# Routed attention and a SERF feed-forward on one core: GpSimd's in-weight forms started three pairs earlier, and the first in-projection's side work laid out anew

## The chip, the core and the metric

The kernel runs on one core of one Trainium2 chip. The core has TensorE (PE; its weight loads are shown as PEld), VectorE (DVE), ScalarE (ACT), GpSimd (POOL) and SyncE (SP), which work through queues of their own and wait for each other by semaphores. The metric is the device time of one execution in microseconds (us). Every profile in this document is of one execution, and times within it are us from the start of its span.

## The reference

Queries and keys are assigned to one of 16 centroids of their head; a query attends to the keys of its own cluster alone. The result is put into rows of 512 numbers and goes through a feed-forward whose activation is h * erf(softplus(h)).

```python
batch, n_heads, seq, head_dim = (4, 8, 768, 64)      # n_clusters = 16
q_assign = np.argmax(np.einsum('bhsd,hcd->bhsc', q_n, c_n), axis=-1)
k_assign = np.argmax(np.einsum('bhsd,hcd->bhsc', k_n, c_n), axis=-1)
mask = q_assign[:, :, :, None] == k_assign[:, :, None, :]
scores = np.where(mask, scale * np.matmul(q, k.transpose(0, 1, 3, 2)), -1000000000.0)
attn = np.exp(scores - np.max(scores, axis=-1, keepdims=True))
attn = attn / (np.sum(attn, axis=-1, keepdims=True) + 1e-09)
x = np.matmul(attn, v).transpose(0, 2, 1, 3).reshape(B * S, H * D)   # 3072 x 512
h = x @ w_in                                          # 512 x 2048
g = h * erf(np.maximum(h, 0.0) + np.log1p(np.exp(-np.abs(h))))
out = g @ w_out                                       # 2048 x 512
```

## The kernel before

**Order of the work.** Nearly every instruction goes through a small class (`InOrder`, L119-132) that records it and keeps each engine in program order; so the profile puts almost all of them on L127, and tiles' names tell them apart. What an engine does next is the order in which the program issues it. DMAs that are issued by `nc.sync` directly are not bound in that way, and stand in SP's queue where the scheduler that builds the program puts them.

**Attention.** 16 pairs of heads (p = 0 to 15), six periods each (i = 0 to 5, `period`, L1367). A period computes scores of two blocks of keys (tile `sc`), their exponentials (ACT, `pr<-sc`), the products with the values (PE, `turned<-pr,in_v`) and, on GpSimd, a running sum of the exponentials (`accumulate`, `more_out<-more_out,pr`). At the end of each half of a pair `divide` (L593) sums that over rows on PE (`turned<-more_out,minus`), takes a reciprocal on ACT (logarithm, exponential), and scales on DVE (`den`, two steps in `turned`, `more_out<-den,turned`); SP stores the result to `x_dram`.

**Weights.** Beside the attention the weights are brought in and made ready for the multiplication by steps that round and rescale them: `fetch` (SP), `size` and `rest` (ACT), `bounded` (DVE), `sign` (ACT), `shifted` (DVE), `summed` (GpSimd, which also issues the next `fetch`). The list `w_steps` (L280) has 16 steps for `w_in`, by column blocks of 512 in the order 0, 512, 1024, 1536, and 16 for `w_out`; pair p finishes steps 2p-2 and 2p-1. The last four (`N_LATE`) are done after the attention, in the first in-projection.

**Forms.** The feed-forward multiplies 2x2 blocks by a scheme of seven products (`ORDER`, L695 and on: 1, 2, 6, 7, 5, 3, 4), which needs sums and differences of blocks of both factors ("forms", 128x512 each). `left_forms` gives four forms for a pair of column blocks f of `w_in`, `right_forms` four for x. In `before`, three groups of four in-weight forms are listed as (DVE, GpSimd) choices; GpSimd takes one from the list in period 1 of each pair named in `POOL_FORMS` (L47: pairs 8 to 15), DVE takes 1, 2, 2 and 2 in periods 0, 3, 4 and 5 of pair 15 (`FORMS`, L46). The four forms of x are put at the end of that list after pair 13; what is left of it goes to DVE behind the loop, and the fourth group of in-weight forms goes to GpSimd behind the attention (L1552).

**First in-projection.** `hidden(0, 0)` and `hidden(0, 1)` (L741) work on one chunk of 512 rows, four column blocks j each, seven products per j. One product is called a block here: four matmul records on PE into one PSUM bank, then one or two operations that add the bank to the results `g`. Blocks are numbered 0 to 55 over both calls. From block 7 on eight banks are used in turn, six of a pool and the two tiles `turned`; in the first seven, six of the pool. For the first product of each j, `hidden(0, 0)` copies by ACT (`first=ae.copy`), `hidden(0, 1)` by DVE. After each block one entry of the list `aside_work` is issued; an `idle` entry is empty. In `before` that list holds: three idle, the four late weight steps (`weights`, sixteen entries), `first_half` (ACT's softplus and erf of half of g, tile `a_s`), `all_sums` (four `summed` on GpSimd), two entries of `middle_forms26` (GpSimd), three idle, the four products `g<-a_s,g` on DVE (`first_products`), and then `second_half`, `late_forms26` (three), four idle, four products. After block 6 `finish_attention` (the rest of the last `divide`) and `next_forms26` are issued. `last_half` is called after the second j of `hidden(0, 1)`: it empties the list and puts in the next half's curves, six idle entries, three left steps and four products.

**Forms of w_out.** The second factor of the out-projection needs its own forms. `early_forms26`, `next_forms26`, `middle_forms26` and `late_forms26` (L816-865) make them on GpSimd in that order; `next_forms26` begins with a tile that `divide` uses until its last step. `late_forms26` ends with two adding DMAs from GpSimd (`onto_by_dma`, `more_out<-x_own`).

**Out-projection.** `project26(0)` (L1236) has 26 products of eight matmul records each, numbered p = 0 to 25 here as in the code. `RIGHT` (L62) says which right factor each takes; values of 100 and over are tiles that are made as it goes (`rest_of_forms26`, L867, by p). Four of them matter below. y0 and y1 (tile `x_own`) are made by a fill or a negation and an adding DMA from GpSimd (`x_own<-more_out`) and also stored by SP (`b_dram<-x_own`). The ring tile used at p = 16 is filled by SP (`g_more<-w_out`, after y0's store in SP's queue) and then added to by GpSimd's DMA (`g_more<-x_own`). The same place is filled again for p = 25 and added to (`g_more<-more_out`).

Of the kernel before, what the change touches and what calls it, by code (L numbers as in the profile page):

```python
# [36 lines left out]
DM, DFF = H * D, 2048  # L37
# [5 lines left out]
LC = 512  # L43

UP = 2.0**16
FORMS = {15: {0: 1, 3: 2, 4: 2, 5: 2}}  # L46
POOL_FORMS = {p: (1,) for p in range(8, 16)}  # L47
BIG = 2.0**60
FLOOR = 2.0**50
EPS = 2.0**-70  # L50
# [1 line left out]
N_LATE = 4  # L52
# [83 lines left out]
def kernel(  # L136
# [141 lines left out]


    w_steps = []  # L280
    for c in range(0, DFF, LC):
        for r in range(DM // P):
            w_steps.append((w_in[:, r, c : c + LC], moe_w_in[r * P : (r + 1) * P, 2 * c : 2 * (c + LC)]))
    for f in range(HF):
# [368 lines left out]
    def left_forms(engine, a11, a12, a21, a22, new):  # L653

        return [
            functools.partial(plus_of, new[0], a21, a22, engine),
            functools.partial(minus_of, new[1], new[0], a11, engine),
            functools.partial(minus_of, a21, a11, a21, engine),
            functools.partial(minus_of, new[2], a12, new[1], engine),
        ]  # L660

    def right_forms(engine, b11, b12, b21, b22, new):

        return [
            functools.partial(minus_of, new[0], b12, b11, engine),
            functools.partial(minus_of, new[1], b22, new[0], engine),
            functools.partial(minus_of, b12, b22, b12, engine),
            functools.partial(minus_of, new[2], new[1], b21, engine),
        ]
# [10 lines left out]
    def w_in_parts(f, n):  # L680
        c1, c2 = slice(f * P, (f + n) * P), slice((HF + f) * P, (HF + f + n) * P)
        return (
            w_in[:, 0:HK, c1], w_in[:, HK:, c1], w_in[:, 0:HK, c2], w_in[:, HK:, c2],
            [more_in[:, i, :, c1] for i in range(3)],
        )

    def x_parts(n):
        x = x_of[n]
        return (
            x[:, 0:HK, 0:HT], x[:, 0:HK, HT:], x[:, HK:, 0:HT], x[:, HK:, HT:],  # L690
            [x_more[:, i] for i in range(3)],
        )
# [4 lines left out]
    aside_work = []  # L697
# [60 lines left out]
    def idle(n):  # L758
        return [lambda: None] * n
# [61 lines left out]
    def next_forms26():  # L821
        w, y = w_block, form_places(1)
        store_form(3, ring[0])
        formed_whole(slot(2), w(5), slot(1), 1)
        formed(y[0], w(3), w(7), -1, 0)
        formed(y[1], w(6), w(7), -1, 0)
        formed(slot(0), w(1), w(7), 1, 0)
# [110 lines left out]
    def split_gate(lot, half):  # L938
        products_of = []

        def curves():
            soft, erf, products = gate26(0, lot, half)
            run(f() for f in soft + erf)
            products_of.extend(products)

        return curves, [lambda i=i: products_of[i]() for i in range(4)]
# [411 lines left out]
            run(steps)  # L1358
        return steps

    forms = []
    for f in range(0, HF - 2, 2):
        forms += zip(*(left_forms(e, *w_in_parts(f, 2)) for e in (ve, ge)))
    routing = [iter(())]
    part = [iter(())]
# [1 line left out]
    def period(p, i):  # L1367
        u = 2 * NJ * p + 2 * i
        n1, n2 = 2 * p - 1, 2 * p
        early = lambda n: 0 <= n < N_EARLY  # L1370

        def mask(place):
            which = (MASKS if p else FIRST_MASKS).get((i, place))
            if which:
                return masks(p + 1, *which, turned[0 if i in (0, 5) else 1], place == 2)
            return lambda: None

        if u > 0:
            for which in turns if i in (0, 3) else ():
                turn(*which)  # L1380
                turns.remove(which)
            if i == 3 and not p:
                transposes(2, "k")
            if i == 3 and p:
                similarities(p + 2)
                routing[0] = choose(p + 2, turned[0], True)
            step_ahead(p, 2 * i)
            if i == 3 and p:
                next(routing[0], None)
            if i == 2:  # L1390
                transposes(p + 2, "k" if p else "q")
        mask(0)()
        if i == 0 and early(n1 - 1):
            sign(n1 - 1)
        elif i == 3 and early(n1):
            sign(n1)
        if i == 4:
            next(routing[0], None)
        next(part[0], None)
        if i == 0 and p:  # L1400
            run(routing[0])
            transposes(p + 2, "q")
        if u == 2:
            next(routing[0])
        products(u)
        mask(3)()
        products(u + 1)
        mask(1)()
        second = step_ahead(p, 2 * i + 1, True) if u > 0 else iter(())
        next(second, None)  # L1410
        rows = D if u == 0 or u + NJ + 2 >= len(units) else Q
        scores(u, rows)
        next(second, None)
        next(second, None)
        next(part[0], None)
        if i == 5 or u == 2:
            next(routing[0], None)
        scores(u + 1, rows)
        later = mask(2)
        if i == 3 and not p:  # L1420
            similarities(p + 2)
            routing[0] = choose(p + 2, turned[0], True)
        if i == 0:
            later()
            curve(u)
        else:
            curve(u)
            later()
        curve(u + 1)
        if u == 0:  # L1430
            step_ahead(0, 1)
            similarities(1)
            routing[0] = choose(1, turned[1])
            next(routing[0])
            vectors(1, "q")
            vectors(1, "k")
        if i == 0 and early(n1 - 1):
            bounded(n1 - 1)
            shifted(n1 - 1)
        elif i == 1 and early(n1):  # L1440
            size_and_rest(n1)
        elif i == 5 and early(n2):
            rest(n2)
        for _ in range(min(len(forms), FORMS.get(p, {}).get(i, 0))):
            forms.pop(0)[0]()
        if i == 3:
            if not p:
                next(routing[0], None)
            if early(n1):
                bounded(n1)  # L1450
                shifted(n1)
        elif i == 1:
            load(p + 1, "v", v, vp)
            if p == 0:
                run(routing[0])
        elif i == 4:
            vectors(p + 2, "k")
            vectors(p + 2, "q")
        if u > 0:
            if i == 1 and early(n1 - 1):  # L1460
                summed(n1 - 1)
            elif i == 4 and early(n1):
                summed(n1)
            if i in POOL_FORMS.get(p, ()) and forms:
                forms.pop(0)[1]()
            for w in (u - 2, u - 1):
                accumulate(w)
            for w in (u - 2, u - 1):
                attend(w)
            if i == 3:  # L1470
                next(routing[0], None)
            if i % HJ == 0:
                part[0] = divide(u - 1)
                next(part[0])
        if i == 3 and early(n2):
            size(n2)
# [61 lines left out]
    for p in range(NPAIR):  # L1538
        for i in range(HJ * 2):
            period(p, i)  # L1540
        if p == LAST_X:
            load_x(0)
        if p == LAST_X + 2:
            forms += zip(*(right_forms(e, *x_parts(0)) for e in (ve, ge)))
    for work, _ in forms:
        work()
    u = len(units)
    for w in (u - 2, u - 1):
        accumulate(w)
    for w in (u - 2, u - 1):  # L1550
        attend(w)
    last = divide(u - 1)  # L1552
    for work in left_forms(ge, *w_in_parts(HF - 2, 2)):
        work()
    attention.close()

    psb = pool("psb", 6, space=PSUM)
# [6 lines left out]
    def finish_attention():  # L1564
        run(last)
        banks[:] = [None] * 6 + turned
# [12 lines left out]
    def weights(n):  # L1579
        return [functools.partial(w, N_EARLY + n) for w in (size_and_rest, bounded, sign, shifted)]  # L1580

    def all_sums():
        for n in range(N_LATE):
            summed(N_EARLY + n)
        take_places(2)

    first_half, first_products = split_gate(0, 0)
    second_half, second_products = split_gate(0, 1)
    aside_work += (
        idle(3) + sum((weights(n) for n in range(N_LATE)), []) + [first_half, all_sums, *middle_forms26(), *idle(3), *first_products]  # L1590
    )
    hidden(0, 0, {0: lambda: (finish_attention(), next_forms26())})

    def last_half():
        finish_aside()
        first_steps = [functools.partial(left_step, 0, x) for x, step in enumerate(LEFT_STEPS) if step[0] < 0]
        aside_work.extend(gate_work(0, 1, 0, first_steps, 6))

    aside_work += [second_half, *late_forms26(), *idle(4), *second_products]
    hidden(0, 1, {1: last_half}, first=ve.tensor_copy)  # L1600
    finish_aside()
    project26(0)
    last_of_x = x_more[:, 2, 0, 0:1]
# [42 lines left out]
```

## Time and profile before

| | |
|---|---|
| median of 3 runs | 950.37 us (950.34 to 950.56) |
| the profiled execution's own time | 950.65 us |
| its span | 948.9 us |
| PE busy, at granted clock 1.0 | 939.7 us |
| DVE, ACT, POOL busy | 789.1, 546.5, 504.6 us |
| attention | about 20 to 401 us |
| first in-projection | about 401 to 452 us |
| first out-projection | about 452 to 497 us |

PE's busy time is from the start of each matmul to a modelled end, so that a busy PE may still be held back; where it matters, the number of matmuls in a stretch is read beside it. In the timeline rows the columns are start, duration, engine, line, operation, result<-operands, shape, count, and in brackets the idle time before the row and what ended it. SPq rows are SP's issues of DMAs, not their transfers.

### The profile page before, as it was taken

To read this page: it belongs to the slowest core of one execution; us is meant where nothing else is said; L and a number is where in the kernel's file an instruction comes from. 1 tells how busy PE (TensorE), PEld (TensorE's weight loads), DVE (VectorE), ACT (ScalarE), POOL (GpSimd) and SP (SyncE) were. 2 spreads that over 40 slices of the span, in tenths; PEclk is the share of its full clock that TensorE was granted. 3 is DMA by queue.
4 is the path that set the end of the run, shared out by engine and by line. 5 is a ranking of instruction groups with operands and counts; after the bars stand their busy time and mean duration, and the time that the engine had idled before them with its cause. 6 is when DMAs were issued, how large, how long until landed. Compare 5 with 4: busy or idle time off the path is not lost.

```text
span 948.9 us, 22319 instructions
## 1 busy us (share of the span) xinstructions
PE 939.7 (99%) x8756; PEld 707.2 (75%) x8756; DVE 789.1 (83%) x1417; ACT 546.5 (58%) x809; POOL 504.6 (53%) x357
## 2 busy tenths in 40 slices
PE   8999999999999999999999999999999999999998
PEld 3555555555555555588888888998999899989987
DVE  8888888888888887879886688688868977897887
ACT  3677777777777776476523643654257236525541
POOL 1688888888888888899108211360063016103600
PEclk9999999999999999999999999999999999999999
DMA  9344554444443621132876347353444336343433
GB/s 220 69 114 113 112 113 113 111 113 111 113 112 68 156 56 36 26 120 112 220 209 248 111 117 203 123 180 111 157 158 143 133 115 209 113 153 123 156 112 111
DMA packets 176344, 123.17 MB, mean 130 GB/s; under 512 B 132592, under 2 KB 143344, under 8 KB 176240
## 3 DMA queue, kind: packets, MB, share of 16 engines
q1 hardware_dynamic: 171872, 116.34, 42.5%
q0 software_dynamic: 1872, 4.98, 2.9%
q8 instruction: 69, 1.13, 0.5%
q10 hardware_dynamic: 2496, 0.43, 0.2%
q14 instruction: 35, 0.29, 0.1%
HBM read 91.78 MB, written 23.33 MB: 121 GB/s over the span
## 4 chain that ended last, share of the span: by engine, by line
PE 93%; DVE 2%; ACT 2%; issue 1%; POOL 1%; DMA 1%; SPq 0%; DVEq 0%; POOLq 0%; ACTq 0%
PE bank L127 40%; PE turned L127 31%; PE sc L127 16%; PE wide L127 6%; POOL more_out L127 1%; DVE nmx L127 1%; DVE g L127 1%; ACT a_s L127 0%; DMA g_more<-in_moe_w_out_dram 0%; ACT L127 0%; ACT osb L127 0%; ACT w_out L127 0%; SPq L127 0%; DMA qm<-least_rows 0%; ACT g_more L127 0%
## 5 line engine op out<-in xcount | busy, mean ns | idle before, releaser
L127 POOL TENSOR_TENSOR more_out<-more_out,pr 128x768 f32<-128x768 f32 x128 | 217.6, 1700 | 17.1 <-ACT pr L127 7.5
L127 DVE TENSOR_REDUCE nmx<-wide 128x2 f32<-128x512 f32 (+2 forms) x189 | 179.1, 948 | 47.1 <-PE wide L127 46.0
L127 ACT ACTIVATE pr<-sc 128x768 f32<-128x768 f32 x192 | 148.4, 810 | 81.3 <-PE wide L127 73.3
L127 PE MATMUL turned<-pr,in_v 128*32 128x193 f32 x3072 | 145.2, 330 | 0.0
L127 POOL TENSOR_TENSOR g<-g 128x512 f32<-128x512 f32 x36 | 47.1, 1309 | 180.8 <-DVE g L127 178.9
L127 PEld LDWEIGHTS turned<-pr,in_v 128*32 128x32 f32 x3072 | 90.2, 109 | 51.3 <-issue 26.9
L127 DVE TENSOR_TENSOR g<-g 128x512 f32<-128x512 f32 x132 | 90.8, 688 | 22.3 <-PE bank L127 11.8
L127 PE MATMUL sc<-qT,kT 64*128 64x384 f32 x528 | 98.5, 485 | 0.0
L127 DVE TENSOR_TENSOR g<-bank,g 128x256 f32<-128x256 f32 (+1 forms) x128 | 64.7, 531 | 16.1 <-PE bank L127 9.5
L127 PE MATMUL bank<-g_more,g 128*128 128x256 f32 x320 | 75.7, 379 | 0.0
L127 PE MATMUL bank<-x_own,w_in 128*128 128x128 f32 (+1 forms) x440 | 74.0, 310 | 0.0
L127 ACT ACTIVATE a_s<-g 128x1024 f32<-128x1024 f32 x38 | 39.5, 1054 | 57.4 <-POOL g L127 45.6
L127 POOL TENSOR_TENSOR more_out<-pr,pr 128x768 f32<-128x768 f32 x32 | 59.1, 1848 | 20.0 <-ACT pr L127 19.9
L127 DVE TENSOR_TENSOR g<-a_s,g 128x512 f32<-128x512 f32 x76 | 68.2, 916 | 0.9 <-ACT a_s L127 0.9
L127 PEld LDWEIGHTS bank<-g_more,g 128*128 128x128 f32 x320 | 60.7, 190 | 8.6 <-DVE g L127 0.4
L127 PEld LDWEIGHTS bank<-x_own,w_in 128*128 128x128 f32 x440 | 63.1, 191 | 4.6 <-issue 0.6
L127 PE MATMUL wide<-kv,qv 64*128 64x256 bf16 (+2 forms) x378 | 64.8, 327 | 0.9 <-ACT km L127 0.6
L127 PE MATMUL bank<-w_out,g 128*128 128x256 f32 x280 | 64.5, 379 | 0.0
L127 ACT ACT_TABLE_LOAD x40 | 51.3, 1283 | 19.8 <-DVE g L127 19.2
L127 PEld LDWEIGHTS <-qv 64*128 64x128 bf16 x384 | 23.1, 93 | 52.7 <-issue 37.9
L127 PE MATMUL wide<-km,qm 64*128 64x256 bf16 (+4 forms) x378 | 62.2, 326 | 0.0
L127 PEld LDWEIGHTS sc<-qT,kT 64*128 64x128 f32 x528 | 46.3, 187 | 19.0 <-issue 2.0
(240 smaller groups left out, 1992.6 us busy)
## 6 DMA issues: line engine op xcount, KB each, us to landing
g_more<-b_dram SPq DMA_DIRECT2D x52, 512.0 KB
g_more<-w_dram SPq DMA_DIRECT2D x84, 256.0 KB
x_own<-in_moe_w_in_dram SPq DMA_DIRECT2D x13, 512.0 KB
in_v<-in_v_dram SPq DMA_DIRECT2D x32, 192.0 KB
x_dram<-more_out SPq DMA_DIRECT2D x128, 48.0 KB
x_own<-x_dram SPq DMA_DIRECT2D x6, 1024.0 KB
in_k<-in_k_dram SPq DMA_DIRECT2D x59, 96.0 KB
in_q<-in_q_dram SPq DMA_DIRECT2D x58, 96.0 KB
```

Source lines behind the costliest of these rows:

```text
L127: ins = getattr(self.engine, name)(*args, **kw)
```

## The change

GpSimd takes one in-weight form in period 1 of pairs 5 to 15 instead of 8 to 15. The order of the `w_in` steps puts columns 0 and 1024 first, so that the first two groups' weights are there earlier. All four groups of in-weight forms are in one list (16), and x's four forms have a list of their own, which DVE takes first in pair 15, followed by three in-weight forms; none is left for DVE behind the loop. The two in-weight forms that remain go to GpSimd behind `next_forms26`; the four that stood before `early_forms26` are gone from there. In the first in-projection the late weight steps begin one block earlier (after block 2), `first_half`, `all_sums` and `middle_forms26` too; the products of the first half stand after blocks 25, 27, 29 and 31 instead of 26 to 29; `second_half` after block 33 instead of 30, `late_forms26` after 34 to 36 instead of 31 to 33, its products after 41, 42, 44 and 45 instead of 38 to 41. `last_half` no longer empties the list and is called one j earlier, so its entries follow the earlier ones: curves after block 46 instead of 42, left steps after 53 to 55 instead of 49 to 51, and the four products after the last block instead of after 52 to 55.

```diff
--- before.py
+++ after.py
@@ -44,7 +44,7 @@
 
 UP = 2.0**16
 FORMS = {15: {0: 1, 3: 2, 4: 2, 5: 2}}
-POOL_FORMS = {p: (1,) for p in range(8, 16)}
+POOL_FORMS = {p: (1,) for p in range(5, 16)}
 BIG = 2.0**60
 FLOOR = 2.0**50
 EPS = 2.0**-70
@@ -278,7 +278,7 @@
 
 
     w_steps = []
-    for c in range(0, DFF, LC):
+    for c in (0, DFF // 2, LC, DFF // 2 + LC):
         for r in range(DM // P):
             w_steps.append((w_in[:, r, c : c + LC], moe_w_in[r * P : (r + 1) * P, 2 * c : 2 * (c + LC)]))
     for f in range(HF):
@@ -1358,8 +1358,8 @@
             run(steps)
         return steps
 
-    forms = []
-    for f in range(0, HF - 2, 2):
+    forms, x_forms = [], []
+    for f in range(0, HF, 2):
         forms += zip(*(left_forms(e, *w_in_parts(f, 2)) for e in (ve, ge)))
     routing = [iter(())]
     part = [iter(())]
@@ -1441,8 +1441,8 @@
             size_and_rest(n1)
         elif i == 5 and early(n2):
             rest(n2)
-        for _ in range(min(len(forms), FORMS.get(p, {}).get(i, 0))):
-            forms.pop(0)[0]()
+        for _ in range(FORMS.get(p, {}).get(i, 0)):
+            x_forms.pop(0)() if x_forms else forms.pop(0)[0]()
         if i == 3:
             if not p:
                 next(routing[0], None)
@@ -1541,17 +1541,13 @@
         if p == LAST_X:
             load_x(0)
         if p == LAST_X + 2:
-            forms += zip(*(right_forms(e, *x_parts(0)) for e in (ve, ge)))
-    for work, _ in forms:
-        work()
+            x_forms += right_forms(ve, *x_parts(0))
     u = len(units)
     for w in (u - 2, u - 1):
         accumulate(w)
     for w in (u - 2, u - 1):
         attend(w)
     last = divide(u - 1)
-    for work in left_forms(ge, *w_in_parts(HF - 2, 2)):
-        work()
     attention.close()
 
     psb = pool("psb", 6, space=PSUM)
@@ -1584,20 +1580,29 @@
             summed(N_EARLY + n)
         take_places(2)
 
+    def spread(work):
+        return sum(([w, *idle(1)] for w in work), [])
+
     first_half, first_products = split_gate(0, 0)
     second_half, second_products = split_gate(0, 1)
     aside_work += (
-        idle(3) + sum((weights(n) for n in range(N_LATE)), []) + [first_half, all_sums, *middle_forms26(), *idle(3), *first_products]
+        idle(2) + sum((weights(n) for n in range(N_LATE)), []) + [first_half, all_sums, *middle_forms26(), *idle(3)]
     )
-    hidden(0, 0, {0: lambda: (finish_attention(), next_forms26())})
+    aside_work += spread(first_products)
+
+    def next_forms():
+        next_forms26()
+        for _, work in forms:
+            work()
+
+    hidden(0, 0, {0: lambda: (finish_attention(), next_forms())})
 
     def last_half():
-        finish_aside()
         first_steps = [functools.partial(left_step, 0, x) for x, step in enumerate(LEFT_STEPS) if step[0] < 0]
         aside_work.extend(gate_work(0, 1, 0, first_steps, 6))
 
-    aside_work += [second_half, *late_forms26(), *idle(4), *second_products]
-    hidden(0, 1, {1: last_half}, first=ve.tensor_copy)
+    aside_work += [second_half, *late_forms26(), *idle(4), *second_products[:2], *idle(1), *second_products[2:]]
+    hidden(0, 1, {0: last_half}, first=ve.tensor_copy)
     finish_aside()
     project26(0)
     last_of_x = x_more[:, 2, 0, 0:1]
```

The order of instructions of the two built programs differs in these ways on top: in SP's queue y1's store now stands ahead of the ring tile's fill in the first out-projection; ACT has `size` and `rest` of the second late step ahead of the last `divide`'s logarithm.

## The prediction

> **What bounds the kernel now.** I read the page first.
>
> ```profile
> PE 939.7 (99%) x8756; PEld 707.2 (75%) x8756; DVE 789.1 (83%) x1417; ACT 546.5 (58%) x809; POOL 504.6 (53%) x357
> ```
>
> TensorE works nearly all the time, so an edit on DVE, ACT or POOL changes the time only where PE waits for it. I therefore looked for such waits in the stages that the change touches, in PE's timeline of the first in-projection and then in DVE's and ACT's.
>
> ```profile
> 431.55 1.03 PE L127 MATMUL bank<-x_more,w_in 128*128 128x256 f32 x4
> 432.41 1.89 PE L127 MATMUL bank<-x_own,w_in 128*128 128x256 f32 x8
> 434.69 1.13 PE L127 MATMUL turned<-x_more,more_in 128*128 128x256 f32 x4 [0.40 <-DVE g L127]
> 436.37 1.13 PE L127 MATMUL turned<-x_own,w_in 128*128 128x256 f32 x4 [0.55 <-DVE g L127]
> 437.34 1.03 PE L127 MATMUL bank<-x_more,more_in 128*128 128x256 f32 x4
> ```
> ```profile
> 426.61 0.42 DVE L127 TENSOR_TENSOR g<-turned,g 128x256 f32<-128x256 f32 x1 [2.91 <-ACT g L127]
> ...
> 434.23 0.41 DVE L127 TENSOR_TENSOR g<-turned,g 128x256 f32<-128x256 f32 x1
> 434.56 1.42 DVE L127 TENSOR_TENSOR g<-a_s,g 128x512 f32<-128x512 f32 x1
> 435.90 0.41 DVE L127 TENSOR_TENSOR g<-turned,g 128x256 f32<-128x256 f32 x1
> ```
> ```profile
> 408.44 0.68 ACT L127 ACTIVATE w_out<-g_more 128x512 f32<-128x512 f32 x1 [3.24 <-DMA g_more<-in_moe_w_out_dram]
> 409.02 2.09 ACT L127 ACTIVATE g_more<-g_more 128x512 int32<-128x512 uint32 x2
> 410.83 0.43 ACT L127 ACTIVATE more_out<-turned,alleps 128x192 f32<-128x192 f32 x1
> ...
> 426.23 0.35 ACT L127 COPY g<-turned 128x256 f32<-128x256 f32 x1
> ```
>
> A block starts 0.86 us after the one before (431.55 to 432.41). From 431.55 to 437.34 lie five blocks (the x8 row is two), so 4.30 us would do where 5.79 pass: **the stall costs 1.49**. PE waits there for evictions of the banks `turned` at 434.23 and 435.90; these are late because DVE first waited 2.91 for ACT's copy at 426.23, and then had one of the products, 1.42, before nearly every eviction. ACT's copy is late because ACT has worked without a gap since the late weights landed at 408.44.
>
> The second chain to watch is GpSimd's, from the attention to the out-projection, and the DMAs behind it.
>
> ```profile
> 404.76 1.72 POOL L127 TENSOR_TENSOR more_in<-w_in 128x512 f32<-128x512 f32 x1
> ...
> 410.26 2.90 POOL L127 TENSOR_TENSOR more_out<-w_out 128x512 f32<-128x512 f32 x2
> ...
> 415.79 2.88 POOL L127 TENSOR_TENSOR more_out<-w_out,more_out 128x512 f32<-128x512 f32 x2
> ...
> 422.70 2.73 POOL L127 TENSOR_TENSOR w_out<-w_out,g_more 128x512 int32<-128x512 int32 x2
> ...
> 449.98 1.86 POOL L127 DMA_DIRECT2D more_out<-x_own  x2
> 459.29 0.84 POOL L127 DMA_DIRECT2D x_own<-more_out  x1 [7.46 <-DMA x_own<-w_out]
> ...
> 473.80 0.84 POOL L127 DMA_DIRECT2D g_more<-x_own  x1 [10.23 <-DMA g_more<-w_out]
> 488.77 0.86 POOL L127 DMA_DIRECT2D g_more<-more_out  x1 [14.14 <-PE bank L127]
> ```
> ```profile
> 463.97 0.32 SPq L794 DMA_DIRECT2D b_dram<-x_own  x1
> ...
> 465.79 1.16 SPq L810 DMA_DIRECT2D g_more<-w_out  x1
> 467.90 0.38 SPq L794 DMA_DIRECT2D b_dram<-x_own  x1
> ...
> 478.29 0.32 SPq L794 DMA_DIRECT2D b_dram<-g_more  x1
> ...
> 494.98 0.32 SPq L794 DMA_DIRECT2D b_dram<-g_more  x1
> ```
> ```profile
> 479.72 1.89 PE L127 MATMUL bank<-g_more,g 128*128 128x256 f32 x8
> ...
> 495.26 1.89 PE L127 MATMUL bank<-g_more,g 128*128 128x256 f32 x8
> ```
>
> POOL has no gap between 404.76 and its DMA issues at 449.98, and then waits only for transfers. SP stores a finished ring tile at 478.29 and 494.98, as soon as it is there. PE takes these tiles at 479.72 (p = 16) and 495.26 (p = 25). So the chain has **1.43 us of slack at p = 16 and 0.28 at p = 25**, and nowhere does PE wait for it yet.
>
> **The change, part by part.** *Three more pairs with a form on GpSimd.* Pair 8 has the first one; a pair without and that pair, and the waits of all six pairs with a form that came to 357 us:
>
> ```profile
> 190.00:213.90 23.90, 23.90 (x348) 12.78 (x340) 20.71 (x36) 18.67 (x30) 19.65 (x13) 1.00 0.48 112
> 213.90:237.80 23.90, 23.90 (x348) 12.70 (x340) 20.72 (x36) 18.63 (x30) 20.82 (x14) 1.00 0.50 113
> ```
> ```profile
> PEld turned L127 <- POOL more_out L127: 1.2, 6, 0.2
> ```
>
> PE starts 348 matmuls in either stretch, so a form costs less than one matmul (23.9 / 348 = 0.07); half of that, three times, is **+0.1**. The bounds are 0, and 3 x 0.2 = 0.6 if each wait of a weight load reached PE. The new order of the `w_in` steps has the same count of instructions and the same owners. DVE still has seven forms in pair 15; I take 0, since PE there waits for a DMA and once for POOL and never for DVE.
>
> *Products spread.* Each of the four products now has two blocks of time, 1.73, against 1.42 for itself and twice 0.41 for evictions: DVE falls behind by 0.51 per product, 2.0 in all, instead of 1.42 + 0.41 - 0.87 = 0.96, or 3.8 in all. 3.8 gave 1.49 of stall, so the banks bear 2.3. By that sum the stall is gone, 1.49 gained. Following the banks by hand I find 0.3 left (block 40 needs the bank of block 32, behind the last product). ACT's work up to the copy is the same, so DVE's 2.91 stays. **-1.2**; the ends are -1.49 and 0 (the stall only moves).
>
> *Late weights one block earlier.* ACT's first step cannot begin before its DMA lands at 408.44, but DVE's step behind it now stands ahead of block 4's eviction.
>
> ```profile
> 409.15 1.44 DVE L127 TENSOR_SCALAR w_out<-w_out 128x512 f32<-128x512 f32 x1 [1.55 <-ACT w_out L127]
> 410.51 0.41 DVE L127 TENSOR_TENSOR g<-bank,g 128x256 f32<-128x256 f32 x1
> ```
> ```profile
> 410.82 1.03 PE L127 MATMUL bank<-x_own,w_in 128*128 128x256 f32 x4
> ```
>
> DVE's queue stands for ACT, and the evictions of blocks 4 and on wait behind it: block 4's two adds end at about 410.51 + 2 x 0.41 = 411.33 instead of before, and block 10, due at 410.82, takes that bank: 411.33 - 410.82 = 0.51, of which I take **+0.4**, as adds in a row close up a little. The ends are 0, if the weights land 0.5 sooner, and 0.6 with a little more at block 14. Both parts together leave PE 0.7 to 0.8 ahead at the end of the in-projection; I go on with 0.7.
>
> *GpSimd's chain.* The four forms of 404.76 to 410.26 are gone, so the early forms of w_out run there instead. But `next_forms26` needs the end of the last `divide`, whose logarithm (410.83) now stands behind one `size` and one of the two instructions of 409.02: 0.58 + 0.90 = 1.48 later. POOL starts 415.79's work no earlier than the division's end, 413.67 (its last DVE step, 413.12 with 0.55) + 1.48 = 415.15 at most, and by 414.8 if the steps on DVE close up.
>
> ```profile
> 413.12 0.55 DVE L127 SCALAR_TENSOR_TENSOR more_out<-more_out,turned 128x384 f32<-128x384 f32 x1
> ```
>
> From there it has five forms, 422.70 - 415.79 = 6.91, and the two in-weight forms, 2.5 to 2.75 (from 404.76 to 410.26 four such took 5.50, with a first one of 1.72). So the work of 422.70 starts between 424.2 and 424.6, **+1.5 to +1.9**, and as nothing has a gap behind it, 449.98 becomes 451.5. The saved 5.5 us of POOL end as idle time ahead of the division. The lower bound of the shift is 0.1, with the logarithm where it was.
>
> Behind that, y0's adding DMA waits for a fill which waits for the slots of 449.98, so it goes from 459.29 to 460.8, and y0's store from 463.97 to 465.5. SP is in order, and in the new program y1's store (467.90) stands ahead of the ring's fill (465.79): one more transfer of 512 KB in front of it.
>
> ```profile
> q0 software_dynamic: 95, 0.39, 96.9%
> ```
> ```profile
> q1 hardware_dynamic: 1069, 2.54, 92.0%
> ```
>
> These are the DMA queues from 463.9 to 466 and from 466 to 474 us: first GpSimd's own adding DMA fills the engines, then SP's transfers run at 2.54 MB in 8 us. One of 0.52 MB takes 0.52 / 2.54 x 8 = 1.6. So the ring's fill lands 1.5 + 1.5 = 3.0 later (nothing to 4.1 if SP also stands for y1), and its adding DMA is issued at 476.8; the finished tile is there at 478.29 + 3.0 = 481.3, with PE due at 479.72 + 0.1 - 0.7 = 479.1. PE waits 2.2. **Behind p = 16 PE is 3.0 - 1.43 = 1.6 late, whatever was gained before it**: the in-projection's gain is swallowed by this wait.
>
> At p = 25 the same place is filled again. The fill stands in SP's queue behind the store of 478.29, so the adding DMA goes from 488.77 to 491.8, and PE is due at 495.26 + 1.6 = 496.9. The trace has these times of adding DMAs, from issue to landing:
>
> ```profile
> g_more<-x_own POOLq DMA_DIRECT2D x1, 512.0 KB, 4.5
> g_more<-more_out POOLq DMA_DIRECT2D x1, 512.0 KB, 6.2
> ```
>
> With 4.5 the tile is there at 496.3, in time; with 6.2 at 498.0, and PE waits 1.1. In the 6.2 most of the last 1.5 us moved almost nothing, so I take the shorter one as likelier, **0**, with +1.1 as the other end.
>
> **Sum**: 950.65 + 0.1 + 1.6 = 952.35 for the profiled execution. That one is 0.28 above the median of 950.37, so the forecast is **952.1**.
>
> **The rivals.** *A, slower again at p = 25.* The adding DMA takes 6.2 as it did in this trace: 952.1 + 1.1 = 953.2. It decides from 496.9 - 491.8 = 5.1 us upwards. For it speaks that this very transfer took 6.2 in the trace; against it that the other one took 4.5.
>
> *B, the chain hides behind PE and the gain stays.* If POOL's shift is small (the logarithm not really later, or the forms of w_in quicker), or y1's store does not hold the fill, the total shift stays under 1.43 - 0.7 = 0.7 and PE never waits. Then the time is 950.37 + 0.1 - 0.7 = 949.8, and 949.0 without the new stalls. Against it: POOL has no gap from 404.76 to 449.98 in which to make up for anything.
>
> *C, the change does not do what it says.* DVE's 2.91 wait for ACT is the root of the stall and stays, so the stall only moves to later blocks; with a small shift of the chain, 950.37 + 0.1 + 0.3 = 950.8.
>
> *D, the ring's adding DMA is quicker than before.* In the trace two of SP's transfers stood behind the ring's fill and moved while this DMA ran; in the new order only one does, and that is nearly done by 476.8. If sharing with it cost the DMA up to one such transfer, 1.6, it takes 2.9 to 4.5, and in the middle, 3.7, all of the 0.8 comes off PE's wait: 951.3. Against it: the other adding DMA took 6.2 at a time when SP had little to move. The page "DMA: Bandwidth & Descriptors" of the Trainium skill (section "Anatomy of one DMA — SWDGE (gpsimd) path") fits a DMA of GpSimd by 2.0 us and its bytes at 436 GB/s, as an estimate 3.2 us for this one, with which the sum would be 1.3 lower, 950.8; the two rows of this trace are longer by 1.3 and 3.0 and speak against it.
>
> **How the numbers follow.** Chances: the forecast 0.40 (952.1), A 0.30 (953.2), B 0.15 (949.8), C 0.07 (950.8), D 0.08 (951.3). The range from 949.5 to 953.9 holds B's main value, and A with half a microsecond of further lateness in SP's queue. About 0.2%, 1.9 us, is what a measurement of this kernel can tell from no change, so faster means below 948.5 and slower above 952.3. Faster would need all of 1.49 and an earlier chain: 0.02. Slower takes A and a small part of the forecast's spread: 0.34. The rest, 0.64, is within 0.2%.
>
> **What would show it.** In the changed kernel's profile: ACT's logarithm near 412.2 and POOL idle for about 4 us ahead of 414.8; the work of 422.70 at about 424.3; no stall of PE at 434 to 437, but 0.4 near 411 in blocks; y1's store ahead of the ring's fill in SP's rows; PE waiting 2 us for a DMA of `g_more` near 481, and the last ring tile landing near 496.5 or 498. If POOL's last forms end where they did, or PE does not wait at p = 16, the prediction is wrong, and the time is that of B; if PE's stall at 434 is still there, C is right.

## The result and the profile after

| | before | changed |
|---|---|---|
| median of 22 runs | 950.38 us (950.06 to 950.93) | 952.04 us (951.26 to 953.75) |
| the profiled execution's own time | 950.65 us | 951.96 us |
| its span | 948.9 us | 950.2 us |

The changed kernel takes 1.0018 of the time before (95% interval 1.0012 to 1.0024): 1.7 us more, where 1.7 more were forecast. Its runs also lie further apart, 2.5 us instead of 0.9.

The page shows nothing of this; PE is as busy as before. What PE waits for, from 100 us to the end, is in the view of its waits (waiting time in total, how often, the longest).

```profile
PE 939.8 (99%) x8756; PEld 707.1 (74%) x8756; DVE 785.5 (83%) x1416; ACT 547.3 (58%) x809; POOL 505.7 (53%) x358
```
```profile
PE bank L127 <- DVE g_more L127: 1.5, 1, 1.5
PE bank L127 <- DMA g_more<-x_own: 0.4, 1, 0.4
PE turned L127 <- POOL more_out L127: 0.3, 1, 0.3
PE sc L127 <- DMA qm<-least_rows: 0.3, 1, 0.3
```

The last two were there before. The second one is the ring tile at p = 16. The first one was not in the prediction. Here is PE's timeline of the changed kernel at these places:

```profile
413.82 1.03 PE L127 MATMUL turned<-x_more,w_in 128*128 128x256 f32 x4
414.99 1.13 PE L127 MATMUL turned<-x_own,w_in 128*128 128x256 f32 x4
...
433.22 1.89 PE L127 MATMUL bank<-x_own,w_in 128*128 128x256 f32 x8
434.95 1.03 PE L127 MATMUL turned<-x_more,more_in 128*128 128x256 f32 x4
435.81 1.03 PE L127 MATMUL turned<-x_own,w_in 128*128 128x256 f32 x4
...
450.49 1.03 PE L127 MATMUL bank<-x_more,w_in 128*128 128x256 f32 x4
453.01 1.96 PE L127 MATMUL bank<-more_out,g_more 128*128 128x256 f32 x8 [1.50 <-DVE g_more L127]
...
478.99 1.89 PE L127 MATMUL bank<-w_out,g 128*128 128x256 f32 x8
481.23 1.97 PE L127 MATMUL bank<-g_more,g 128*128 128x256 f32 x8 [0.36 <-DMA g_more<-x_own]
...
496.85 1.89 PE L127 MATMUL bank<-g_more,g 128*128 128x256 f32 x8
```

The old stall is gone: the two blocks in `turned` follow at 0.86 us. Block 14 starts 0.31 late (414.99 instead of 413.82 + 0.86): its bank is one of the tiles `turned`, in which the late division still works, up to the end of DVE's row here.

```profile
414.38 0.56 DVE L127 SCALAR_TENSOR_TENSOR more_out<-more_out,turned 128x384 f32<-128x384 f32 x1
```

Then PE stands still for 1.50 us ahead of the first product of the out-projection, which needs the second left step, and for 0.36 ahead of p = 16. p = 16 starts at 481.23, against 479.72 before: 1.51 late; p = 25 is 1.59 late (496.85 against 495.26), and at the end of the span 1.3 are left.

GpSimd's queue in the changed kernel, and SP's:

```profile
407.61 2.52 POOL L127 TENSOR_TENSOR g_more<-w_out 128x512 f32<-128x512 f32 x2
415.07 2.76 POOL L127 TENSOR_TENSOR more_out<-w_out,more_out 128x512 f32<-128x512 f32 x2 [4.95 <-DVE more_out L127]
...
424.72 2.54 POOL L127 TENSOR_TENSOR w_out<-w_out,g_more 128x512 int32<-128x512 int32 x2
...
449.35 2.97 POOL L127 TENSOR_TENSOR more_out<-w_out,g_more 128x512 f32<-128x512 f32 x2
452.25 1.89 POOL L127 DMA_DIRECT2D more_out<-x_own  x2
...
476.61 0.84 POOL L127 DMA_DIRECT2D g_more<-x_own  x1 [13.29 <-DMA g_more<-w_out]
491.29 0.86 POOL L127 DMA_DIRECT2D g_more<-more_out  x1 [13.84 <-DMA g_more<-w_out]
```
```profile
466.82 0.33 SPq L794 DMA_DIRECT2D b_dram<-x_own  x1
...
470.20 0.32 SPq L794 DMA_DIRECT2D b_dram<-x_own  x1
470.69 0.63 SPq L810 DMA_DIRECT2D g_more<-w_out  x1
...
481.11 0.32 SPq L794 DMA_DIRECT2D b_dram<-g_more  x1
```

GpSimd stands idle for 4.95 us until the division ends, and from there every step is late: 2.0 at 424.72 (422.70 before), 2.3 at 452.25 (449.98), 2.8 at 476.61 (473.80). The finished tile is there at 481.1 instead of 478.3. SP's fill of it goes out 4.9 later (470.69 against 465.79), because SP stood until 470.20 for y1, whose store is now ahead of it. From the fill's issue to GpSimd's DMA it then took 5.9 instead of 8.0.

### The profile page after: what moved, and what is told of

It reads as the page before. It is cut to its first block, busy times and chain, and to the rows that moved or that the text cites. A ratio compares the mean times of both kernels' runs of the same rounds, so it can differ in the third digit from the quotient of the medians.

```text
span 950.2 us, 22316 instructions
## 1 busy us (share of the span) xinstructions
PE 939.8 (99%) x8756; PEld 707.1 (74%) x8756; DVE 785.5 (83%) x1416; ACT 547.3 (58%) x809; POOL 505.7 (53%) x358
## 4 chain that ended last, share of the span: by engine, by line
PE 94%; DVE 2%; DMA 2%; POOL 1%; issue 1%; ACT 1%; SPq 0%; DVEq 0%; POOLq 0%; ACTq 0%
PE bank L127 41%; PE turned L127 31%; PE sc L127 16%; PE wide L127 6%; DVE nmx L127 1%; POOL more_out L127 1%; DMA g_more<-w_out 1%; DMA g_more<-x_own 0%; DMA g_more<-in_moe_w_out_dram 0%; DVE g_more L127 0%; SPq L127 0%; DMA qm<-least_rows 0%; DVE more_out L127 0%; ACT w_out L127 0%; DVE turned L127 0%
## 5 line engine op out<-in xcount | busy, mean ns | idle before, releaser
L127 DVE TENSOR_TENSOR g<-a_s,g 128x512 f32<-128x512 f32 x76 | 65.3, 880 | 0.5 <-ACT a_s L127 0.5
```

Of the source, the lines that this page charges most:

```text
L127: ins = getattr(self.engine, name)(*args, **kw)
```

## The experiments

Two theories. **One**: the ring tile at the end of GpSimd's chain sets the time at p = 16; whatever the in-projection gains or loses ahead of it is swallowed. **Two**: the end of the in-projection (the 1.5 us of waiting for the left step) sets it, and the tile's lateness happens to fit. All times are medians; ratios are to the kernel before on the same chip.

**Left steps earlier.** In the changed kernel:

```
-        aside_work.extend(gate_work(0, 1, 0, first_steps, 6))
+        aside_work.extend(gate_work(0, 1, 0, first_steps, 2))
```

> The changed kernel with the three left steps of the last curves moved from behind blocks 53 to 55 to behind 49 to 51, where they were before. Theory one (the chain of GpSimd's forms and DMAs sets the time at p = 16): PE's wait of 1.50 us for DVE at the start of the out-projection goes, PE is due at p = 16 about 1.5 earlier, near 479.4, and waits for the same ring tile near 481.1, so 0.4 becomes 1.9; the time stays at 952.0 (951.3 to 952.8). Theory two (the end of the in-projection sets it, the ring tile is a coincidence): 952.0 - 1.5 = 950.5.

953.21 us, ratio 1.0032 (1.0021 to 1.0044): slower than the changed kernel, though a wait of 1.5 us is gone. Theory two, which says 950.5, falls. Theory one is right about the place and misses the size (951.3 to 952.8). Two things are new. First, PE's timeline at the tile, and the windows around it (the columns are the stretch, its length, busy time and count of instructions of PE, PEld, DVE, ACT and POOL, then granted clock, DMA share and GB/s):

```profile
477.82 1.89 PE L127 MATMUL bank<-w_out,g 128*128 128x256 f32 x8
481.80 3.28 PE L127 MATMUL bank<-g_more,g 128*128 128x256 f32 x8 [2.10 <-DMA g_more<-x_own]
484.88 2.31 PE L127 MATMUL bank<-more_out,g_more 128*128 128x256 f32 x8
487.02 1.89 PE L127 MATMUL bank<-g_more,g 128*128 128x256 f32 x8
```
```profile
480.00:482.00 2.00, 0.20 (x1) 0.23 (x2) 1.80 (x4) 0.56 (x2) 0.00 (x0) 1.00 0.55 102
482.00:485.00 3.00, 3.00 (x9) 2.40 (x9) 0.00 (x0) 0.00 (x0) 0.00 (x0) 0.55 0.83 287
485.00:488.00 3.00, 3.00 (x14) 2.57 (x13) 2.03 (x4) 0.38 (x1) 0.00 (x0) 0.88 0.99 312
```

After 2.10 us without a matmul **the granted clock falls to half for about 3 us**: from 482 to 485 only nine matmuls start (16 in the changed kernel). Two products take 5.22 us (481.80 to 487.02) instead of 3.45 (479.72 to 483.17 before): another 1.8 us, on top of the wait. The six runs fall into 952.4 to 952.5 (three) and 953.9 to 954.5 (three), about that distance apart. The mean granted clock on record for each run divides them in the same way: 0.998 in the three long ones, of which the profiled one (954.36) is one, and 1.0 in the three short ones; half the clock for 3.4 of 952 us is a mean of 0.998. So the fall came in half of the executions. The three short ones lie within the spread of the changed kernel. The Trainium skill, page "TensorE: Matmul & The Clock Gate", section on the clock gate in Part 1, has the clock fall after an idle window of about 3.4 us, free-running, and return after a busy one. In the profiled run here 2.1 us of idling were enough, the half clock lasted about as long as that window, and 1.50 us in the changed kernel did not do it.

Second, GpSimd was later still: its DMA issue stood at 453.37 (452.25 in the changed kernel), mostly because its last four forms took 2.95 and 3.40 a pair instead of 2.51 and 2.97; DVE's three left steps now ran beside them, and took 1.34, 1.42 and 1.43 each.

**Two forms in the gap.** In the changed kernel the two in-weight forms go ahead of `next_forms26`:

```
     def next_forms():
-        next_forms26()
         for _, work in forms:
             work()
+        next_forms26()
```

> The changed kernel with the two in-weight forms on GpSimd ahead of next_forms26, in the gap where GpSimd waits for the last divide, instead of behind it. Theory one: GpSimd's work behind them starts 2.9 us earlier, its adding DMA 452.25 goes to about 449.4, the ring tile of p = 16 is there near 478.3 and PE's wait of 0.36 is gone; the time is 951.6, and its spread over the runs shrinks to that of the kernel before, since no DMA is waited for. Theory two: 952.0, no change, the spread too.

950.76 us, ratio 1.0004 (0.9995 to 1.0013), runs 950.34 to 951.0. GpSimd's chain is as early as forecast (449.18, the tile's DMA at 474.02), the wait at p = 16 is gone and the spread is down to 0.7, as theory one has it. But 1.3 came off, where 0.4 were expected. PE's wait at the start of the out-projection was halved as well. The timelines of DVE and PE, first of this kernel, then DVE's of the changed one:

```profile
451.29 0.68 DVE L127 TENSOR_TENSOR g_more<-g,g_more 128x512 f32<-128x512 f32 x1
```
```profile
452.12 1.97 PE L127 MATMUL bank<-more_out,g_more 128*128 128x256 f32 x8 [0.74 <-DVE g_more L127]
```
```profile
451.43 1.43 DVE L127 TENSOR_TENSOR g_more<-g,g_more 128x512 f32<-128x512 f32 x1
```

The same left step takes 0.68 when GpSimd's forms are over (449.18), and 1.43 while the last of them runs (449.35 to 452.25, above). This is the left step before it in the changed kernel:

```profile
450.50 0.68 DVE L127 TENSOR_TENSOR g_more<-g 128x512 f32<-128x512 f32 x1
```

The second form of the pair at 449.35 runs from 450.57 to 452.31. The step that began 0.07 ahead of it took 0.68, and the form 1.74, where the first of the pair took 1.27. The step that began inside it (451.43) ended at 452.86, 0.55 behind its end. The kernels with the left steps earlier and with both edits show the same 0.55: it looks as if a step begun inside a form is held until the form ends. So GpSimd's lateness cost twice: at the tile, and at this step.

**Both edits.**

> Both edits at once. Theory one: both waits of PE go together, 952.0 - 0.4 - 1.5 = 950.1 (949.6 to 950.5), though each edit alone gave little. Theory two: the sum of what the two gave alone, 950.5 if the left steps gave 1.5.

949.71 us, ratio 0.9994 (0.9985 to 1.0003). PE reaches p = 16 at 479.05 and waits for nothing there; it waits 0.42 at p = 25. Left steps moved by themselves cost 1.2; with GpSimd's chain in time they gain 1.05. That is theory one: what an edit ahead of a late transfer gives depends on the transfer.

**y1's store out of SP's queue.** In the changed kernel ACT issues it, behind p = 10:

```
-        def work(f, *args):
-            return functools.partial(f, *args)
+        def work(f, *args, **kw):
+            return functools.partial(f, *args, **kw)
...
-                work(store_form, 4, y[1]),
...
+            10: [work(ae.dma_start, out=stored_form(4), in_=y[1])],
```

> The changed kernel with y1's store issued by ACT behind p = 10, so that the ring tile's fill stands directly behind the other fill in SP's queue, as before the change. Theory one as predicted (1.5 of the ring tile's 3.0 us of lateness is y1's store ahead of its fill): the fill lands 1.5 to 2.9 earlier, the tile of p = 16 is there near 479.7 and PE does not wait, 951.6 to 951.7. Rival (all of the lateness comes down GpSimd's queue): tile near 481, 952.0.

951.49 us, ratio 1.0012 (1.0003 to 1.0021), runs 951.22 to 951.72: as forecast within 0.2. The tile's DMA goes out at 475.07 instead of 476.61, 1.54 earlier, near the 1.5 of the prediction. GpSimd's lateness alone (this kernel, whose DMA issue is at 452.42) moves it from 473.80 to 475.07, 1.3; the store's place alone (the two forms in the gap, or the layout alone, below) moves it hardly, to 474.02 or 473.67 (DMA issue at 449.18 and 449.91); the two together give 2.8.

**The forms alone, and the layout alone.** The first takes from the change only the forms, the second only the side work's layout.

The diff of the forms alone against the changed kernel:

```diff
-    aside_work += (
-        idle(2) + sum((weights(n) for n in range(N_LATE)), []) + [first_half, all_sums, *middle_forms26(), *idle(3)]
-    )
-    aside_work += spread(first_products)
...
+    aside_work += (
+        idle(3) + sum((weights(n) for n in range(N_LATE)), []) + [first_half, all_sums, *middle_forms26(), *idle(3), *first_products]
+    )
...
     def last_half():
+        finish_aside()
...
-    aside_work += [second_half, *late_forms26(), *idle(4), *second_products[:2], *idle(1), *second_products[2:]]
-    hidden(0, 1, {0: last_half}, first=ve.tensor_copy)
+    aside_work += [second_half, *late_forms26(), *idle(4), *second_products]
+    hidden(0, 1, {1: last_half}, first=ve.tensor_copy)
```

The layout alone is the kernel before with these lines the other way round.

> Only the first half of the change: GpSimd's in-weight forms from pair 5, the order of the weight steps, x's forms first on DVE, and the two in-weight forms behind next_forms26; the side work of the in-projection stays as before the change. Theory one (only the lateness of the ring tile against PE counts): the attention is 0.4 longer as in the changed kernel, the stall at 434 to 437 stays, the division ends near 414.1, GpSimd's chain is 1.4 later and the tile of p = 16 is there near 479.7 with PE due at 480.1; no wait, 950.8, at most 951.5 if the tile of p = 25 takes 6.2 again. Theory two (the moved forms cost the whole of it): 952.0.

> Only the second half of the change: the side work laid out anew, GpSimd's forms as before. Theory one: no stall at 434 to 437 but 1.5 us of waiting for the left steps at the start of the out-projection, PE due at p = 16 0.5 later than before; GpSimd has its four forms to do while the division ends, so its chain is not shifted and only y1's store delays the tile, to 479.6, before PE is there; 950.9. The two halves give 0.4 and 0.5 alone and 1.66 together. Theory two (layout alone makes the chain late): 951.6 to 952.0.

950.75 us, ratio 1.0005 (0.9996 to 1.0013), and 950.78 us, 1.0005 (0.9996 to 1.0014). Both times are as forecast: p = 16 starts at 480.21 and 480.13 (480.1 and 480.2 expected), without a wait. The ways to them are not, so that these two hits are in part luck. With the forms alone, the stall at 434 to 437 was 0.7 instead of 1.5, and PE waited 0.63 ahead of the out-projection, because the first left step took 1.70 beside GpSimd's last form. With the layout alone, the wait for the left steps was 0.74 instead of 1.5, but block 10 came 0.48 late, because the weights' bounding step took 1.45 beside GpSimd's four forms. And the tile of p = 16 was stored at 477.8 and 478.2, where 479.7 and 479.6 were expected and 478.3 was measured before the change: neither half makes it late at all. Alone they cost 0.4 each, together 1.7.

**The logarithm early.** In the changed kernel an empty entry moves between the first two late weight steps, so that the division's logarithm comes ahead of the second, as before the change.

```
-        idle(2) + sum((weights(n) for n in range(N_LATE)), []) + [first_half, all_sums, *middle_forms26(), *idle(3)]
+        idle(2) + weights(0) + idle(1) + sum((weights(n) for n in range(1, N_LATE)), []) + [first_half, all_sums, *middle_forms26(), *idle(2)]
```

> The changed kernel with the second late weight step behind the last divide's logarithm, as before the change (one empty entry moved ahead of it); with that the built program also has y1's store behind the ring tile's fill again. Theory one: logarithm near 411.2 instead of 412.33, GpSimd's work of 415.07 near 413.9, the tile of p = 16 at about 478.5 to 479, no wait of PE for it; the wait of 1.5 us for the left steps stays, 951.6. Theory two (the division's lateness is not passed on): GpSimd's DMA issue still near 452.2, 951.6 at best through the store alone.

950.85 us, ratio 1.0006 (0.9998 to 1.0015). In the run y1's store stood ahead of the ring's fill all the same, so the logarithm is the only difference. It starts at 411.12 (412.33 in the changed kernel), GpSimd goes on at 413.89 (415.07), its DMA issue is at 450.74 (452.25), and PE does not wait at p = 16. The division's lateness is passed on in full, which theory one says. Of the 0.8 gained beyond the forecast, 0.4 is block 14's lateness, which is gone (the last block starts at 450.10 instead of 450.49), and 0.2 the shorter wait ahead of the out-projection, 1.30; the left step there took 0.67 again. The other 0.2 was not traced.

**Three, four and five edits.** The first has left steps earlier, the two forms in the gap and y1's store by ACT; the second also the early logarithm; the third also no form on GpSimd in pair 12, and so three in the gap:

```
-POOL_FORMS = {p: (1,) for p in range(5, 16)}
+POOL_FORMS = {p: (1,) for p in range(5, 16) if p != 12}
```

> Left steps earlier, the two forms in the gap, and y1's store by ACT, all three. Theory one: in the kernel with the first two PE still waits 0.42 us for the tile of p = 25, which comes down SP's queue; with y1's store out of that queue the fill is 1.3 earlier and this wait goes too: 949.71 - 0.4 = 949.3 (949.1 to 949.6). Rival (the wait is the transfer's own length): 949.7.

> The kernel of three edits (left steps earlier, two forms in the gap, y1's store by ACT) with the second late weight step behind the division's logarithm as a fourth. Theory one: with no wait for a ring tile left, what counts are PE's own small waits; the 0.19 at the block of 414.5 goes with this step, 949.68 - 0.2 = 949.5. Rival (the earlier chain itself still gives time): 949.0 or less.

> The same four edits, and no form on GpSimd in pair 12, which took 24.23 us in the changed kernel and 23.91 before; three in-weight forms instead of two then run in GpSimd's gap behind the attention. If that form is what makes pair 12 longer, the pair goes back to 23.9 and the time to 949.5 - 0.3 = 949.2. Rival (the 0.3 comes from something else in that pair, or moves to another pair): 949.5, with another pair of 24.2.

949.68 us (ratio 0.9993, 0.9984 to 1.0002), 949.26 us (0.9988, 0.9979 to 0.9997) and **948.88 us (0.9984, 0.9975 to 0.9993)**. The first gained nothing on the kernel of two edits: the 0.42 at p = 25 is gone from its profile, but the median is the same. The profiled execution of the kernel of two edits was its longest (950.39, 0.7 above the median), so the wait need not be in the others; no run settles it. The other two did what was expected or a little more, and the last beats the kernel before by 1.5 us. Pair 12, in the windows of the changed kernel and of this one:

```profile
309.20:333.60 24.40, 24.28 (x348) 12.88 (x347) 21.21 (x37) 18.84 (x29) 21.06 (x14) 1.00 0.61 154
```
```profile
309.20:333.60 24.40, 24.40 (x360) 13.19 (x356) 21.23 (x37) 19.18 (x30) 20.14 (x13) 1.00 0.63 154
```

With 14 instructions on GpSimd 348 matmuls start, with 13 360; the pair's period goes from 24.23 to 23.90 us. Before the change GpSimd had 14 in this pair too and the pair took 23.91, so it is not the load alone. What the form meets is the division of that pair, which takes GpSimd's running sum. This is its weight load, before and in the changed kernel:

```profile
322.68 0.16 PEld L127 LDWEIGHTS turned<-more_out,minus 128*32 128x32 f32 x8 [0.18 <-POOL more_out L127]
```
```profile
323.09 0.16 PEld L127 LDWEIGHTS turned<-more_out,minus 128*32 128x32 f32 x8 [0.50 <-POOL more_out L127]
```

GpSimd's step ahead of the form starts at 311.66 instead of 311.28, because it waits for ACT's `inv` instead of `pr`; the sum ends at 323.03 instead of 322.64, and the load waits 0.32 longer. Without the form the step is as late, but the sum ends 1.4 earlier and the load does not wait. PE's waits in this kernel from 100 us on are the two old ones:

```profile
PE turned L127 <- POOL more_out L127: 0.3, 1, 0.3
PE sc L127 <- DMA qm<-least_rows: 0.3, 1, 0.3
```

## Why the prediction was right, point by point

- **Three more pairs, +0.1.** The first block starts 0.38 later (401.81 against 401.43). Some 0.1 is the pairs' own, 0.3 is pair 12, where one wait of a weight load reached PE. The term was too small; the bound of 0.6, which was made of such waits, held.
- **Products spread, -1.2.** The stall went whole, with nothing left at block 40: -1.49.
- **Late weights earlier, +0.4 at block 10.** Block 10 was on time, for the weights' bounding step took 0.92 instead of 1.44, with GpSimd idle from 410.13 on. In the layout alone, where GpSimd is busy there, the step took 1.45 and block 10 was 0.48 late, as forecast: the prediction left out that its own change of the forms shortens this step. A cost of 0.31 came at block 14 instead, from the late division and not from the evictions behind the weights. With all this the last block starts at 450.49 instead of 451.23, 0.74 ahead; 0.6 to 0.7 was forecast.
- **What the prediction did not have**: the left steps. They moved behind blocks 53 to 55, the first product of the out-projection needs the second of them, and PE waited 1.50. The change's own order said so; the prediction followed the products and not these.
- **GpSimd's chain, +1.5 to +1.9, then 3.0 at the tile.** Logarithm 412.33 (412.2 forecast), GpSimd at 415.07 (414.8), 424.72 (424.2 to 424.6), DMA issue 452.25 (451.5), tile at 481.1 (481.3). The steps between were later than forecast and the transfers closer together: 2.3 at the DMA issue instead of 1.5 (the prediction went on with the low end of its +1.5 to +1.9), and 0.5 more behind it instead of 1.5 (for that transfer it had worked out 1.6). SP did stand for y1, which the prediction had only in its bound of 4.1. That the sum of 3.0 came out at 2.8 is in part luck. The experiments with the logarithm, the gap and y1's store each remove the wait at p = 16, so that the tile's lateness comes down GpSimd's queue and through y1's store is shown, not only argued.
- **PE's wait at p = 16, 2.2.** It was 0.4, because PE came 1.0 late by itself instead of 0.6 early. The start was right, 481.23 for 481.3, and with it the time: only the tile decides it. But the wait of 2.2 was priced as 2.2. Had PE come as early as forecast, it would have idled as long as in the kernel with the left steps earlier, where the clock fell in half of the runs; by that kernel's runs, the time would have been 952.4 to 954.5. **An error in one step (the left steps) hid an omission in another (the clock).**
- **p = 25.** Its adding DMA took the shorter time, and the tile was stored at 496.04, 0.8 before PE came; rival A did not occur in this execution. Its mechanism is real: in the profiles of the other kernels this DMA took 4.8 to 6.4, and in the kernel of both edits it took 6.1 and PE waited 0.42 for it. Whether it occurred in others of the 22 runs is not on record. These are the changed kernel's rows:

```profile
g_more<-x_own POOLq DMA_DIRECT2D x1, 512.0 KB, 4.5
g_more<-more_out POOLq DMA_DIRECT2D x1, 512.0 KB, 4.7
```

- **Rivals.** B falls: the chain was 2.8 late, not 0.7. C falls: DVE still waited for ACT's copy (1.81) and no stall followed. D falls: the adding DMA took 4.5, as before; the fit on the Trainium skill's page "DMA: Bandwidth & Descriptors" (section "Anatomy of one DMA — SWDGE (gpsimd) path"), by which 3.2 us is the estimate, is not borne out by any adding DMA of 512 KB here. That the runs lie 2.5 us apart fits a tile that PE just waits for: in the kernels without that wait they lie 0.5 to 1.0 apart.

## What to carry to other kernels

When an edit delays a chain of another engine, follow it to the next point where the bounding engine takes something from it, and compare arrival with arrival there; what is gained or lost ahead of that point does not add to the sum. Look for idle time that the edit itself opens on the late engine: moving two forms into GpSimd's new gap of 4.95 us gave back 1.3 of the 1.7 us lost. And read where every moved entry lands, not only those that the stall in question is made of.

## What the runs showed of the hardware

- TensorE's granted clock fell to 0.50 after 2.10 us without a matmul and stayed there for about 3 us, at a cost of 1.8 us, in three of six runs of that kernel; after 1.50 and 0.74 us of idling it stayed at 1.00.
- One and the same 128x512 step on DVE took 0.68 us with GpSimd idle and 1.43 us when it began inside a GpSimd form, ending 0.55 us behind the form; a form took 1.74 us instead of 1.27 when DVE's step began 0.07 us ahead of it.
